# Scores of two attention batches in seven chunks of 128 queries instead of eight of 120

## The chip, the cores and the metric

The kernel runs on one core of a Trainium2 chip. The metric is the time of one execution on the device, in microseconds (us). Before the change the median of three runs was 487.84 us, the lowest 485.43 and the highest 489.74.

## The reference

One attention block with head mixing, then two feed-forward blocks. Everything is fp32, with batch B = 2, H = 12 heads, S = 448 tokens and D = 64 per head.

```
scores = einsum('bhij,hg->bgij', q @ k^T / 8, w_pre)      # mix heads
attn   = softmax(scores, axis=-1)
attn   = einsum('bhij,hg->bgij', attn, w_post)            # mix heads again
x      = (attn @ v) as [B, S, 768]
u      = x + (relu(x^T @ w_tok1) @ w_tok2)^T              # over tokens
x      = u + relu(u @ w_ch1) @ w_ch2                      # over channels
h      = gelu(x @ w_in);  u, v = halves of h
out    = x + (u * (w_sg @ layernorm(v) + b_sg)) @ w_out
```

The change touches only how the raw scores q @ k^T are cut and when their operands are loaded.

## The kernel before, in words

**Scores (`qk`).** The 448 queries of a batch are cut into chunks of 120, 120, 120 and 88, so there are eight chunks for the two batches. For each of them `qk(x, i)` computes chunk x of head pair i: TensorE (PE) multiplies the q columns of the chunk with k of that pair (lines 326 to 329), and one copy on ScalarE (ACT) or VectorE (DVE) takes the result, 128 x 896, out of PSUM into the chunk's S tile (line 333). A call costs the same for the chunk of 88 queries as for one of 120, since the 128 columns of the q tile are filled up with zeros. There are 8 x 6 = 48 calls. S tiles live in three places: one named S3 and two that rotate.

**Steps.** The mixing works on 20 queries at a time: there are 23 steps for each batch, 46 in all, numbered over both batches. For step i:

- `b_dma` gathers the scores from S into two ring tiles P: 10 queries x 12 heads land on 120 partitions. Such a tile is one DMA on the queue of SyncE (SP), and reads 10 rows of S that lie 12 partitions apart. The ring has 8 tiles, four steps' worth. P of step i + 5 is sent in step i, in steps 14 and 16 one step more (`LONG`).
- `b_pre` mixes heads (PE, "pre"), `b_max` finds the negated maximum (DVE, "nm", line 373), `b_exp` exponentiates (ACT, "E", line 381): these three are issued two steps ahead (`LP` = 2).
- `b_norm` forms the weights from the sums (GpSimd, POOL, "wt"), one step ahead.
- `b_post` mixes heads again on PE ("post"), and `b_turn` copies the result into AT, on DVE, in five steps on ACT (line 433).

Two pairs of PSUM banks (`psB`) hold pre; two others (`psM`) are shared in turn by `qk`, post and `av`.

**What lies between the steps.** `av` multiplies AT with v, for two chunks at a time, in steps 12, 14, 16, then 23, 25, 27, then 35, 36, 40 and later. In the middle of `av`, PE waits for a small POOL instruction (`turned_at`, line 474), which in turn waits for the first matmuls of `av`. `QK_AT` gives the step in which each `qk` call stands; in a step the order is pre, `qk`, post, `av` on PE. `CONV` says how many instructions of a conversion of weights are issued in a step: first right after `b_norm`, then after `b_turn` and before `av`, then at the end of the step. Each of four early weight pieces goes through |x| on ACT, a clamp on POOL (line 132), three bit operations on DVE (lines 134, 136, 138), a copy on ACT and a subtraction on POOL. Its raw tile (`eraw`) has one buffer, so the load of the next piece waits on SP until the third DVE operation is done. The list `loads` names the step in which q, k and v are loaded, all on the SP queue in the order of the program.

**After the steps** come the feed-forward blocks, nearly all matmul, and their weights' loads and conversions; they follow the attention part in program order and are not touched by the change.

Of the kernel before, what the change touches and what calls it, by code (L numbers as in the profile page):

```python
# [21 lines left out]
NP_BUFS = 2 * (LD - LP + 1)  # L22
# [3 lines left out]
V_EARLY = {7: 0, 11: 1, 15: 2, 19: 3}  # L26

GATE_ORDER = "u0 u1 v4 u2 v5 u3"


@with_exitstack
def tile_kernel(ctx, tc, q, k, v, w_pre, w_post, w_tok1, w_tok2, w_ch1, w_ch2,
                w_u, w_v, g_ln, w_sg, b_sg, w_out, out):
    nc = tc.nc
    B, D, H, S = 2, 64, 12, 448
    P = 128
    NP = H // 2
# [7 lines left out]
    IB = 10  # L45
    TILES = P // IB
# [235 lines left out]
    def big(nm, dt=F32R):  # L282
        return sp_.tile([P, SWC], dt, tag="S", name=nm, bufs=2)
# [22 lines left out]
    def load_q(b, c, g, eng=nc.sync):
        t = qn[b, c, g] = qp.tile([P, QG, P], F32, tag=f"qn{g}", name=f"qn{b}_{c}_{g}", bufs=2)
        eng.dma_start(out=t, in_=q[b, :, c, g * QG:(g + 1) * QG])

    KG = [(i, 1) for i in range(NP)]  # L310

    def load_k(b, g):
        i, n = KG[g]
        x = qp.tile([P, n, S], F32, tag=f"kn{g}", name=f"kn{b}_{g}")
        nc.sync.dma_start(out=x, in_=k[b, :, i:i + n])
        for j in range(n):
            KX[b, i + j] = x[:, j]

    def qk(x, i, pool=psM, copies=(nc.scalar.copy,)):

        b, c = chunks[x]
        if i == 0:
            SS[b, c] = qp.tile([P, SWC], F32, tag="S3", name=f"S{b}_{c}") if x % 3 == 1 else big(f"S{b}_{c}", F32)
        nm = f"qk{b}_{c}_{i}"
        ps = pair(nm, pool)
        for cols in HALVES:
            for j, rows in enumerate(HALVES):
                nc.tensor.matmul(ps[cols, j, :S], lhsT=qn[b, c, i // QG][rows, i % QG, cols], rhs=KX[b, i][rows],  # L328
                                 start=True, stop=True)
        n = 2 // len(copies)  # L330
        for j, copy in enumerate(copies):
            o = (2 * i + j * n) * S
            copy(SS[b, c][:, o:o + n * S].rearrange("p (j s) -> p j s", j=n), ps[:, j * n:(j + 1) * n, :S])  # L333


    steps = []
# [11 lines left out]
    PAD = 64 - HW  # L348
    NK = S // 64

    ring = [ap_.tile([P, S], F32, name=f"P{n}") for n in range(NP_BUFS)]

    def b_dma(i):

        b, c, p, ne = steps[i]
        for r in range(2):
            t = 2 * p + r
            ni = IB if ne == 2 else HB
            src = SS[b, c][t:t + (ni - 1) * TILES + 1:TILES]
            nc.sync.dma_start(out=ring[(2 * i + r) % NP_BUFS][PAD:PAD + ne * HW], in_=src)  # L360

    def b_pre(i):
        ne = steps[i][3]
# [155 lines left out]
        extra.setdefault(step, []).append((fn, a))  # L519

    chunks = [(b, c) for b in range(B) for c in range(len(CH))]
    NCH = len(chunks)
    starts = set(first.values())


    load_k(0, 0)
    load_q(0, 0, 0, nc.scalar)
    for g in range(1, len(KG)):
        load_k(0, g)
        if g == 2:  # L530
            load_q(0, 0, 1)
    for g in range(NQ):
        load_q(0, 1, g)
    load_const()
    load_v(0, 0)

# [33 lines left out]
    for at, fn, *a in [(1, load_q, 0, 3, 0), (5, load_q, 0, 3, 1), (9, load_k, 1, 0), (10, load_q, 1, 0, 0), (11, load_k, 1, 1),   # L570
                       (12, load_v, 0, 1), (12, load_k, 1, 2), (12, load_k, 1, 3), (12, load_q, 1, 0, 1), (14, load_v, 0, 2),
                       (14, load_k, 1, 4), (14, load_k, 1, 5), (14, w_dma), (14, load_const_late),
                       (16, load_q, 1, 1, 0), (16, load_q, 1, 1, 1), (18, load_q, 1, 2, 0), (20, load_q, 1, 2, 1), (25, load_v, 1, 0), (25, load_q, 1, 3, 0),
                       (27, load_v, 1, 1), (27, load_q, 1, 3, 1), (35, load_v, 1, 2)]:
# [381 lines left out]
def layouts(q, k, v, w_pre, w_post, moe_w_tok1, moe_w_tok2, moe_w_ch1, moe_w_ch2,  # L956
            moe2_w_in, moe2_g_ln, moe2_w_sg, moe2_b_sg, moe2_w_out):

    import numpy as np

    def bits(a):

        return a.view(np.uint64) if a.dtype == np.float64 else a

    def rows(a, p):

        return bits(a).reshape(-1, p, a.shape[1]).transpose(1, 0, 2)

    def blocks(a):

        n = a.shape[0] // 128 * 128
        return rows(np.concatenate([a, a[n:]]), 128)

    def cols(a, p):

        return bits(a).reshape(a.shape[0] // p, p, -1, p).transpose(1, 2, 0, 3)

    def diagonal(w):
        h = w.shape[0]
# [5 lines left out]
    def spread(a):

        n = a.shape[-1]
        full, rest = n // 10, n % 10
        a = a.reshape(*a.shape[:-1], 2, n // 2)
        a = np.concatenate([a, np.zeros((*a.shape[:-1], -(n // 2) % 5), a.dtype)], -1)  # L990
        a = a.reshape(*a.shape[:-1], -1, 5)
        t = np.zeros((*a.shape[:-3], 128), a.dtype)
        rows = t[..., :120].reshape(*a.shape[:-3], 2, 5, 12)
        rows[..., :full] = a[..., :full, :].swapaxes(-1, -2)
        if rest:
            rows[..., 0, :, full:full + 2] = a[..., full, :].swapaxes(-1, -2)
        t[..., :120] = rows.reshape(*a.shape[:-3], 120)
        return t
# [8 lines left out]
    qt = np.stack([spread(qt[..., s:s + 120]) for s in range(0, S, 120)], 2)  # L1007
# [27 lines left out]
    return {n: np.ascontiguousarray(a) for n, a in arrays.items()}  # L1035
# [34 lines left out]
```

## Time and profile before

| | |
|---|---|
| median of three runs | 487.84 us (485.43 to 489.74) |
| the profiled execution's own time | 486.01 us |
| its span, first to last instruction | 484.2 us |
| PE busy | 470.1 us, 97% |
| DVE, ACT, POOL busy | 70%, 48%, 44% |
| granted TensorE clock | 1.0 of full speed throughout |

The times of instructions are microseconds from the span's start. The steps of the attention part run from 14 us to 165 us; what follows lasts to 484 us. "Idle before" in a row of the timeline is how long the engine had nothing to do before that instruction, and after the arrow stands what ended the idle time. Matmul ends are modelled, so a PE that shows as busy may still issue more slowly than it could. "issue" means that no wait shows in the profile. 1.8 us of the 486.01 lie outside the span.

### The profile page before, as it was taken

To read this page: it belongs to the slowest core of one execution; us is meant where nothing else is said; L and a number is where in the kernel's file an instruction comes from. 1 tells how busy PE (TensorE), PEld (TensorE's weight loads), DVE (VectorE), ACT (ScalarE), POOL (GpSimd) and SP (SyncE) were. 2 spreads that over 40 slices of the span, in tenths; PEclk is the share of its full clock that TensorE was granted. 3 is DMA by queue.
4 is the path that set the end of the run, shared out by engine and by line. 5 is a ranking of instruction groups with operands and counts; after the bars stand their busy time and mean duration, and the time that the engine had idled before them with its cause. 6 is when DMAs were issued, how large, how long until landed. Compare 5 with 4: busy or idle time off the path is not lost.

```text
span 484.2 us, 12943 instructions
## 1 busy us (share of the span) xinstructions
PE 470.1 (97%) x5476; PEld 386.8 (80%) x5476; DVE 340.3 (70%) x453; ACT 232.3 (48%) x453; POOL 212.8 (44%) x305
## 2 busy tenths in 40 slices
PE   8979999999999999999999999999999999999997
PEld 4555555566657899999999999999999998888896
DVE  3779556757765568536577767888779855898882
ACT  3767667678764454533344342324333343555320
POOL 2266545756654203831233331655544450358400
PEclk9999999999999999999999999999999999999999
DMA  7656765385635014022243343324333233004222
GB/s 254 238 207 216 274 229 188 112 271 189 231 139 203 5 39 146 12 66 70 104 140 111 134 160 130 132 93 146 132 110 108 85 79 121 21 0 131 81 91 102
DMA packets 26302, 64.17 MB, mean 133 GB/s; under 512 B 2900, under 2 KB 19844, under 8 KB 26244
## 3 DMA queue, kind: packets, MB, share of 16 engines
q1 hardware_dynamic: 26100, 63.14, 38.2%
q8 instruction: 43, 0.70, 0.6%
q10 hardware_dynamic: 144, 0.20, 0.1%
q14 instruction: 15, 0.12, 0.1%
HBM read 41.22 MB, written 2.75 MB: 91 GB/s over the span
## 4 chain that ended last, share of the span: by engine, by line
PE 87%; ACT 3%; issue 3%; DVE 3%; POOL 2%; DMA 2%; POOLq 0%; ACTq 0%; SPq 0%; DVEq 0%
PE qk L328 7%; PE c1ps L673 6%; PE c2ps L673 6%; PE pre L368 6%; PE c2ps L675 6%; PE c1ps L675 6%; PE c2ps L674 6%; PE c1ps L674 6%; PE av L482 6%; PE post L415 5%; PE ups L674 2%; PE ups L673 2%; PE ups L675 2%; PE vps L675 2%; PE vps L673 2%
## 5 line engine op out<-in xcount | busy, mean ns | idle before, releaser
L157 POOL TENSOR_TENSOR wl<-cv,wh 128x768 fp32r<-128x768 f32 x28 | 53.1, 1898 | 124.4 <-ACT wh L154 92.7
L415 PEld LDWEIGHTS post<-wt,E 60*64 60x64 f32 x2520 | 45.3, 134 | 28.1 <-issue 12.3
L381 ACT ACTIVATE E<-pre,nm 128x448 f32<-128x448 f32 x90 | 56.5, 637 | 14.6 <-DVE nm L373 13.0
L415 PE MATMUL post<-wt,E 60*64 60x60 f32 x2520 | 48.5, 219 | 4.9 <-issue 3.5
L136 DVE SCALAR_TENSOR_TENSOR cv<-raw,cv 128x768 uint32<-128x768 uint32 (+2 forms) x44 | 51.5, 1171 | 1.3
L673 PE MATMUL c2ps<-r1h,wh 128*128 128x448 f32 x144 | 52.3, 363 | 0.0
L673 PE MATMUL c1ps<-uh,wh 128*128 128x448 f32 x144 | 52.3, 363 | 0.0
L675 PE MATMUL c2ps<-r1h,wl 128*128 128x448 f32 x144 | 52.2, 362 | 0.0
L675 PE MATMUL c1ps<-uh,wl 128*128 128x448 f32 x144 | 52.2, 362 | 0.0
L674 PE MATMUL c2ps<-r1l,wh 128*128 128x448 f32 x144 | 51.9, 360 | 0.0
L674 PE MATMUL c1ps<-ul,wh 128*128 128x448 f32 x144 | 51.8, 360 | 0.0
L433 DVE COPY AT<-post 128x840 f32<-128x840 f32 x40 | 41.3, 1032 | 14.5 <-PE post L415 14.5
L373 DVE TENSOR_REDUCE nm<-pre 128x2 f32<-128x896 f32 (+1 forms) x46 | 48.9, 1063 | 2.3 <-PE pre L368 2.2
L114 ACT ACTIVATE cv<-raw 128x768 f32<-128x768 f32 (+2 forms) x44 | 36.2, 823 | 28.4 <-POOL wl L157 20.7
L333 ACT COPY S<-qk 128x896 f32<-128x896 f32 x40 | 36.1, 906 | 22.9 <-PE qk L328 22.7
L328 PE MATMUL qk<-kn,qn 64*64 64x448 f32 x384 | 45.7, 555 | 1.5 <-DMA qn<-in_q_dram 1.5
L368 PE MATMUL pre<-P,wp 64*64 64x448 f32 (+1 forms) x360 | 46.1, 539 | 0.3 <-ACT E L381 0.3
L138 DVE SCALAR_TENSOR_TENSOR cv<-raw,cv 128x768 uint32<-128x768 uint32 (+2 forms) x44 | 41.9, 952 | 1.1
L154 ACT CAST wh<-cv 128x768 fp32r<-128x768 f32 x28 | 23.4, 836 | 34.8 <-DVE cv L138 33.8
L696 DVE SCALAR_TENSOR_TENSOR r1l<-c1ps,r1h 128x448 fp32r<-128x448 f32 x24 | 15.0, 623 | 30.6 <-ACT r1h L694 30.6
L134 DVE TENSOR_SCALAR cv<-cv 128x768 uint32<-128x768 uint32 (+2 forms) x44 | 30.4, 692 | 6.8 <-POOL turned_at L474 3.0
L390 POOL TENSOR_TENSOR rr<-rc,mone 128x2 f32<-128x2 f32 (+1 forms) x46 | 33.4, 726 | 3.8
(151 smaller groups left out, 997.1 us busy)
## 6 DMA issues: line engine op xcount, KB each, us to landing
P<-S SPq DMA_DIRECT2D x88, 210.0 KB
raw<-in_w_ch_dram SPq DMA_DIRECT2D x24, 768.0 KB
vn<-in_v_dram SPq DMA_DIRECT2D x6, 512.0 KB
raw<-in_w_v_dram SPq DMA_DIRECT2D x6, 512.0 KB
raw<-in_w_u_dram SPq DMA_DIRECT2D x4, 768.0 KB
raw<-in_w_out_dram SPq DMA_DIRECT2D x6, 512.0 KB
qn<-in_q_dram SPq DMA_DIRECT2D x15, 192.0 KB
kn<-in_k_dram SPq DMA_DIRECT2D x12, 224.0 KB
```

The lines of the kernel that those rows point to most:

```text
L136: nc.vector.scalar_tensor_tensor(fi, lo, 29, fi, op0=ALU.logical_shift_right, op1=ALU.bitwise_or)
L138: nc.vector.scalar_tensor_tensor(fi, hi, 0xC0000000, fi, op0=ALU.bitwise_and, op1=ALU.bitwise_or)
L157: nc.gpsimd.tensor_tensor(dst[1], f, f32(dst[0]), op=ALU.subtract)
L328: nc.tensor.matmul(ps[cols, j, :S], lhsT=qn[b, c, i // QG][rows, i % QG, cols], rhs=KX[b, i][rows], start=True, stop=True)
L368: nc.tensor.matmul(ps[cols, e, :S], lhsT=wp[rs], rhs=ring[(2 * i + r) % NP_BUFS][rs], start=True, stop=True)
L373: nc.vector.tensor_reduce(out=st[i]["nm"][:, :ne], in_=st[i]["pre"][:, :ne, :S], axis=AX.X, op=ALU.max, negate=True)
L381: nc.scalar.activation(t, st[i]["pre"][:, e, :S], AF.Exp, bias=st[i]["nm"][:, e:e + 1], scale=1.0, accum_out=sm[:, e:e + 1])
L415: nc.tensor.matmul(ps[HALVES[x], r, o:o + HW], lhsT=st[i]["e"][e][rs, t * 64:(t + 1) * 64], rhs=st[i]["w"][e][rs, :HW], start=True, stop=True)
L433: copy(dst, src)
L673: nc.tensor.matmul(ps, lhsT=lh, rhs=rh, start=(start and i == 0), stop=False)
L674: nc.tensor.matmul(ps, lhsT=lh, rhs=rl, start=False, stop=False)
L675: nc.tensor.matmul(ps, lhsT=ll, rhs=rh, start=False, stop=(stop and i == n - 1))
```

## The change

The queries of both batches are laid in one row of 896 and cut into seven chunks of 128. Chunk 3 holds the last 64 queries of batch 0 and the first 64 of batch 1, so its `qk` calls take k of both batches. There are 7 x 6 = 42 calls. The steps stay as they were. A P tile whose 10 queries lie in two chunks is gathered by two DMAs; `score_rows` lists the places. This happens for the tiles whose queries are split 8 + 2, 6 + 4, 4 + 6 (batch 0) and 4 + 6, 2 + 8 (batch 1): 97 gathers in place of 92. In batch 0 the last five whole tiles read rows 5 partitions apart, in batch 1 the first six read rows 6 apart; the pieces of a split tile, and the two short tiles at the end of each batch, read neighbouring rows. The two short tiles are 48 rows of P in place of 60.

While chunk 3 is computed, k of both batches must be held. The first three pairs of k of batch 1 are loaded into tiles that the weight conversion uses later (`eraw` and `ecv`, "lent"), the other three over pairs of batch 0 that are done; the first three are loaded a second time in steps 16 and 17. k is then loaded in steps 7, 9, 10, 11, 12, 12, 16, 16, 17 instead of 9, 11, 12, 12, 14, 14, one load of q chunk (two DMAs) falls away, and the conversions move from steps 15 to 42 into steps 22 to 41. The host's reordering of q follows `score_rows`.

The core of the diff:

```
     def load_k(b, i, home):
+        if home < 0:
+            if not lent:
+                lent[0] = ap_.tile([P, 2 * EC], U32, tag="eraw", name="lent0").bitcast(F32)
+                lent[1] = ap_.tile([P, EC], F32, tag="ecv", name="lent1")
+            x = (lent[0][:, :S], lent[0][:, EC:EC + S], lent[1][:, :S])[home]
+        else:
+            x = qp.tile([P, S], F32, tag=f"kn{home}", name=f"kn{b}_{i}")
+        nc.sync.dma_start(out=x, in_=k[b, :, i])
+        KX[b, i] = x
...
-        for cols in HALVES:
+        for h, cols in enumerate(HALVES):
...
-                nc.tensor.matmul(ps[cols, j, :S], lhsT=qn[b, c, i // QG][rows, i % QG, cols], rhs=KX[b, i][rows],
+                nc.tensor.matmul(ps[cols, j, :S], lhsT=qn[x, i // QG][rows, i % QG, cols],
+                                 rhs=KX[(2 * x + h) // NCH, i][rows], start=True, stop=True)
...
         for r in range(2):
-            t = 2 * p + r
-            ni = IB if ne == 2 else HB
-            src = SS[b, c][t:t + (ni - 1) * TILES + 1:TILES]
-            nc.sync.dma_start(out=ring[(2 * i + r) % NP_BUFS][PAD:PAD + ne * HW], in_=src)
+            to = PAD
+            for x, a, by, n in places(b, c, 2 * p + r):
+                src = SS[x][a:a + (n - 1) * by + 1:by]
+                nc.sync.dma_start(out=ring[(2 * i + r) % NP_BUFS][to:to + n * H], in_=src)
+                to += n * H
...
-    QK_AT = [[-2, -2, -1, -1, 0, 1], [3, 5, 7, 9, 11, 12], [13, 14, 14, 15, 16, 17], [18, 18, 19, 20, 21, 22], [23, 24, 25, 26, 27, 28], [29, 30, 31, 32, 33, 34]]
+    QK_AT = [[-2, -2, -1, -1, 0, 1], [9, 11, 12, 13, 14, 14], [15, 16, 17, 18, 19, 20], [21, 22, 23, 24, 25, 26], [28, 29, 30, 31, 32, 33]]
...
-    CONV = {15: (0, 0, 2), 16: (0, 3, 0), 18: (1, 0, 0), 19: (0, 1, 0), 21: (0, 1, 0), 22: (1, 1, 0), 23: (0, 2, 0), 25: (0, 0, 1), 26: (1, 0, 0), 27: (2, 3, 0), 29: (0, 1, 0), 30: (1, 0, 0), 36: (1, 1, 0), 38: (1, 0, 1), 39: (0, 1, 0), 40: (1, 0, 0), 42: (0, 0, 1)}
-    RAW_AT = (16, 23, 27)
+    CONV = {22: (0, 0, 1), 23: (1, 3, 1), 24: (1, 0, 0), 25: (1, 0, 1), 27: (0, 3, 1), 28: (1, 0, 0), 35: (1, 0, 1), 36: (0, 3, 1), 37: (1, 0, 0), 39: (0, 0, 1), 40: (1, 3, 1), 41: (1, 0, 0)}
+    RAW_AT = (17, 23, 27, 36)
```

`qk` calls therefore disappear from steps 3, 5, 7, 27 and 34, and step 18 keeps one of its two; every other step from 9 to 33 keeps the number that it had.

## Rows read from the trace of the kernel before

**Rows 1.** The page: busy time of each engine, and the chain's shares.
```profile
PE 470.1 (97%) x5476; PEld 386.8 (80%) x5476; DVE 340.3 (70%) x453; ACT 232.3 (48%) x453; POOL 212.8 (44%) x305
PE 87%; ACT 3%; issue 3%; DVE 3%; POOL 2%; DMA 2%; POOLq 0%; ACTq 0%; SPq 0%; DVEq 0%
```

**Rows 2.** The page's groups: busy us, mean ns of one | idle before, releaser.
```profile
L373 DVE TENSOR_REDUCE nm<-pre 128x2 f32<-128x896 f32 (+1 forms) x46 | 48.9, 1063 | 2.3 <-PE pre L368 2.2
L433 DVE COPY AT<-post 128x840 f32<-128x840 f32 x40 | 41.3, 1032 | 14.5 <-PE post L415 14.5
...
L333 ACT COPY S<-qk 128x896 f32<-128x896 f32 x40 | 36.1, 906 | 22.9 <-PE qk L328 22.7
L328 PE MATMUL qk<-kn,qn 64*64 64x448 f32 x384 | 45.7, 555 | 1.5 <-DMA qn<-in_q_dram 1.5
```

**Rows 3.** Windows: stretch, length, PE, PEld, DVE, ACT, POOL busy, clock, DMA, GB/s.
```profile
25.35:45.53 20.18, 17.18 (x548) 11.04 (x544) 16.30 (x17) 14.14 (x39) 12.30 (x33) 1.00 0.57 205
67.84:74.81 6.97, 5.77 (x116) 3.58 (x116) 4.47 (x7) 3.03 (x8) 5.69 (x10) 1.00 0.50 154
74.81:78.43 3.62, 3.26 (x84) 1.62 (x77) 2.62 (x3) 3.20 (x7) 0.96 (x3) 1.00 0.32 122
104.26:106.58 2.32, 2.32 (x76) 1.39 (x72) 1.87 (x3) 2.07 (x5) 1.01 (x1) 1.00 0.66 234
106.58:112.51 5.93, 5.72 (x116) 3.46 (x113) 2.91 (x7) 3.97 (x10) 5.23 (x10) 1.00 0.59 175
124.39:129.29 4.90, 4.12 (x140) 2.93 (x139) 3.27 (x4) 3.49 (x8) 3.07 (x8) 1.00 0.49 185
165.00:484.00 319.00, 315.12 (x1702) 289.57 (x1697) 230.59 (x320) 123.56 (x198) 124.06 (x89) 1.00 0.29 97
```

**Rows 4.** Timeline, 23 to 33 us: start, length, instruction, count [idle before].
```profile
23.48 0.49 SPq L308 DMA_DIRECT2D qn<-in_q_dram  x1
...
28.16 0.98 PE L328 MATMUL qk<-kn,qn 64*64 64x448 f32 x8 [0.80 <-DMA qn<-in_q_dram]
...
32.87 0.63 PE L415 MATMUL post<-wt,E 60*64 60x60 f32 x28 [1.79 <-issue]
```

**Rows 5.** Timeline around the `av` of step 16.
```profile
67.80 0.69 ACT L114 ACTIVATE cv<-raw 128x512 f32<-128x512 f32 x1
...
68.57 1.93 POOL L132 TENSOR_SCALAR cv<-cv 128x512 f32<-128x512 f32 x1 [4.82 <-ACT cv L114]
...
69.33 0.44 PE L464 MATMUL av<-AT,vn 64*64 64x120 f32 x8 [0.50 <-ACT S L333]
...
73.05 0.44 PE L464 MATMUL av<-AT,vn 64*64 64x120 f32 x8 [0.70 <-POOL turned_at L474]
```

**Rows 6.** Timeline of PE, steps 26 and 27.
```profile
105.83 0.94 PE L328 MATMUL qk<-kn,qn 64*64 64x448 f32 x8
106.58 1.00 PE L415 MATMUL post<-wt,E 60*64 60x60 f32 x56
107.79 0.44 PE L464 MATMUL av<-AT,vn 64*64 64x120 f32 x8 [0.21 <-ACT S L333]
```

**Rows 7.** Timeline, steps 33 to 35.
```profile
125.57 0.85 PE L415 MATMUL post<-wt,E 60*64 60x60 f32 x43 [0.78 <-issue]
...
128.84 1.04 DVE L433 COPY AT<-post 128x840 f32<-128x840 f32 x1 [0.29 <-PE post L415]
...
130.10 0.32 PE L464 MATMUL av<-AT,vn 64*64 64x120 f32 x3
```

**Rows 8.** Timeline of the SP queue's gathers and loads, and two `qk` calls.
```profile
19.98 3.45 SPq L360 DMA_DIRECT2D P<-S  x4
...
36.70 1.63 SPq L360 DMA_DIRECT2D P<-S  x2
...
42.69 1.02 PE L328 MATMUL qk<-kn,qn 64*64 64x448 f32 x8
...
45.66 0.47 SPq L308 DMA_DIRECT2D qn<-in_q_dram  x1
...
49.69 0.96 PE L328 MATMUL qk<-kn,qn 64*64 64x448 f32 x8
```

More of the change, by code (lines that the diff above doesn't have):

```diff
@@ L28, with score_rows @@
 GATE_ORDER = "u0 u1 v4 u2 v5 u3"
+def score_rows():
+    S, IB, P = 448, 10, 128
+    got = []
+    for b in range(2):
+        sizes = [IB] * (S // IB) + [S % IB // 2] * 2
+        at, rows = b * S, [[] for _ in sizes]
+        t = done = 0
+        while t < len(sizes):
+            room = P - at % P
+            left = sizes[t] - done
+            full = 0
+            while not done and sizes[t] == IB and t + full < S // IB and (full + 1) * IB <= min(room, (b + 1) * S - at):
+                full += 1
+            if full:
+                for n in range(full):
+                    rows[t + n].append((at + n, full, IB))
+                at += full * IB
+                t += full
+                continue
+            n = min(left, room)
+            rows[t].append((at, 1, n))
+            at += n
+            done += n
+            if done == sizes[t]:
+                t, done = t + 1, 0
+        got.append(rows)
+    return got
 @with_exitstack
@@ L299, in tile_kernel @@
     QG = 3
+    NCH = B * S // P
     NQ = NP // QG
@@ L304, in load_v, with load_q, load_k @@
         nc.sync.dma_start(out=t, in_=v[b, :, g])
[L306 to L317, printed above, removed]
+    def load_q(x, g, eng=nc.sync):
+        t = qn[x, g] = qp.tile([P, QG, P], F32, tag=f"qn{g}", name=f"qn{x}_{g}", bufs=2)
+        eng.dma_start(out=t, in_=q[x, :, g * QG:(g + 1) * QG])
+    lent = {}
+    def load_k(b, i, home):
+        if home < 0:
[7 more added lines that the diff above has]
+        KX[b, i] = x
     def qk(x, i, pool=psM, copies=(nc.scalar.copy,)):
-        b, c = chunks[x]
         if i == 0:
-            SS[b, c] = qp.tile([P, SWC], F32, tag="S3", name=f"S{b}_{c}") if x % 3 == 1 else big(f"S{b}_{c}", F32)
-        nm = f"qk{b}_{c}_{i}"
-        ps = pair(nm, pool)
-        for cols in HALVES:
+            SS[x] = qp.tile([P, SWC], F32, tag="S3", name=f"S{x}") if x % 3 == 0 else big(f"S{x}", F32)
+        ps = pair(f"qk{x}_{i}", pool)
+        for h, cols in enumerate(HALVES):
             for j, rows in enumerate(HALVES):
-                nc.tensor.matmul(ps[cols, j, :S], lhsT=qn[b, c, i // QG][rows, i % QG, cols], rhs=KX[b, i][rows],
-                                 start=True, stop=True)
+                nc.tensor.matmul(ps[cols, j, :S], lhsT=qn[x, i // QG][rows, i % QG, cols],
+                                 rhs=KX[(2 * x + h) // NCH, i][rows], start=True, stop=True)
         n = 2 // len(copies)
@@ L332, in qk @@
             o = (2 * i + j * n) * S
-            copy(SS[b, c][:, o:o + n * S].rearrange("p (j s) -> p j s", j=n), ps[:, j * n:(j + 1) * n, :S])
+            copy(SS[x][:, o:o + n * S].rearrange("p (j s) -> p j s", j=n), ps[:, j * n:(j + 1) * n, :S])
     steps = []
@@ L349, in tile_kernel, with places @@
     NK = S // 64
+    def places(b, c, t):
+        return [(n // P, n % P, by, m) for n, by, m in score_rows()[b][TILES * c + t]]
     ring = [ap_.tile([P, S], F32, name=f"P{n}") for n in range(NP_BUFS)]
@@ L521, in tile_kernel @@
     chunks = [(b, c) for b in range(B) for c in range(len(CH))]
-    NCH = len(chunks)
     starts = set(first.values())
[L526 to L531, printed above, removed]
+    load_k(0, 0, 0)
+    load_q(0, 0, nc.scalar)
+    for i in range(1, NP):
+        load_k(0, i, i)
+        if i == 2:
+            load_q(0, 1)
     for g in range(NQ):
-        load_q(0, 1, g)
+        load_q(1, g)
     load_const()
@@ L567, in tile_kernel @@
     for g in range(NQ):
-        load_q(0, 2, g)
+        load_q(2, g)
     loads = {}
[L570 to L574, printed above, removed]
+    for at, fn, *a in [(1, load_q, 3, 0), (5, load_q, 3, 1), (7, load_k, 1, 0, -3), (9, load_k, 1, 1, -2), (10, load_q, 4, 0), (10, load_k, 1, 2, -1),
+                       (11, load_k, 1, 3, 0), (12, load_k, 1, 4, 1), (12, load_v, 0, 1), (12, load_k, 1, 5, 2), (12, load_q, 4, 1), (14, load_v, 0, 2),
+                       (14, load_const_late), (16, load_k, 1, 0, 3), (16, load_k, 1, 1, 4), (16, load_q, 5, 0), (17, load_k, 1, 2, 5),
+                       (18, load_q, 5, 1), (25, load_v, 1, 0), (23, load_q, 6, 0),
+                       (27, load_v, 1, 1), (25, load_q, 6, 1), (35, load_v, 1, 2)]:
         loads.setdefault(at, []).append((fn, a))
@@ L590, in tile_kernel @@
     todo = []
-    for x in range(0, NCH - 2, 2):
+    for x in range(0, len(chunks) - 2, 2):
         f0, f1 = first[chunks[x + 2]], first[chunks[x + 3]]
         for m in range((NP // 2)):
-            todo.append((f0 + (MID_AT[m] if x + 4 == NCH else m * (f1 - f0) // (NP // 2)), chunks[x:x + 2], (2 * m, 2 * m + 1)))
+            todo.append((f0 + (MID_AT[m] if x + 4 == len(chunks) else m * (f1 - f0) // (NP // 2)), chunks[x:x + 2], (2 * m, 2 * m + 1)))
     for m, hps in enumerate(LAST):
@@ L983, in diagonal @@
         return t
[L985 to L998, printed above, removed]
     def tokens(w):
@@ L1006, in layouts @@
     qt = q.reshape(B, H // 2, 2, S, D).transpose(0, 2, 4, 1, 3).reshape(B, 2 * D, H // 2, S)
-    qt = np.stack([spread(qt[..., s:s + 120]) for s in range(0, S, 120)], 2)
+    order = np.zeros(B * S, int)
+    for b, tiles in enumerate(score_rows()):
+        for t, segments in enumerate(tiles):
+            c, j = t // 12, t % 12
+            n = min(120, S - 120 * c)
+            rows_at = np.concatenate([np.arange(a, a + by * m, by) for a, by, m in segments])
+            i = np.arange(len(rows_at))
+            if t < S // 10:
+                order[rows_at] = b * S + 120 * c + i // 5 * (n // 2) + 5 * j + i % 5
+            else:
+                r = t - S // 10
+                order[rows_at] = b * S + 120 * c + r * (n // 2) + n // 10 * 5 + i
+    qt = qt.transpose(1, 2, 0, 3).reshape(2 * D, H // 2, B * S)[..., order].reshape(2 * D, H // 2, -1, 128).transpose(2, 0, 1, 3)
     whole = S // 128 * 128
```

## The prediction

> **What bounds the kernel now.** I read the page's busy lines first, then the groups by operation, then windows laid over single stretches, then the timeline inside them. PE is busy 97% of the span and carries 87% of the chain [rows 1], and after 165 us PE is busy for 315.12 of 319.00 us [rows 3]. The change takes nothing out of that part, so it only starts earlier by whatever the attention part gives up; the whole gain or loss must be found between 14 and 165 us. There a busy PE is not enough to go by. A plain step with one `qk` call takes 2.32 us (the window from 104.26 [rows 3]), and PE is recorded busy through all of it. But DVE needs 1.063 us for its maximum and 1.032 us for the copy into AT [rows 2], 2.10 us for every step, call or no call. So a call taken out of a plain step can give at most about 0.22 us before DVE sets the pace, though its PE slot is 0.75 us long (105.83 to 106.58 [rows 6]). The first stretch shows the same: eight steps in 20.18 us [rows 3], less the idle 0.80 and 1.79 us [rows 4], are 2.20 us a step, although about half of them have a call. Six calls at 45.7 us / 48 = 0.95 us of PE each [rows 2], 5.7 us, is therefore not the forecast; each call is worth what its own step can give.
>
> **The six calls that go.**
>
> Step 3: PE stands 0.80 us for the q chunk whose load went out at 23.48 [rows 4]. In the new order that chunk is first used in step 9, so the wait goes. Soon after, PE is idle 1.79 us with no wait that the profile names [rows 4]; if that idle time hangs on the clock on the wall and not on the work before it, it swallows the gain. Bounds 0 and 0.8; I take 0.7, since a wait that is named is gone for certain and the other is not known to move. Next late there is DVE.
>
> Steps 3, 5, 7: from 2.20 to at best 2.10 us over the eight steps, 0.8 at most, 0 at least; I take 0.3.
>
> Step 18: two calls in one step make 3.62 us (the window from 74.81 [rows 3]), a step with one 2.32. Gain 1.3; a second call in a step is pure PE and ACT time (its copy takes 0.906 us [rows 2]), and DVE is busy only 2.62 of the 3.62.
>
> Step 27: here `av` follows. The call's slot is 0.75 us, and `av` then waits 0.21 us more, because it takes over the call's PSUM pair and must wait for its copy [rows 6]. Without the call it follows post directly: 0.96 us. DVE is busy 2.91 of 5.93 us in the `av` stretch (the window from 106.58 [rows 3]) and doesn't step in. I take 1.0; lower bound 0.2, if DVE's pace carries through.
>
> Step 34: before the last steps without calls, two steps last 4.90 us (the window from 124.39 [rows 3]), of which 0.78 is idle without a named cause [rows 7]. `av` starts at 130.10, 0.2 us after the copy into AT that ends at 129.88 [rows 7], so DVE is again close behind. Bounds 0.2 and 0.75 + 0.78 = 1.5; I take 0.6, nearer the end that DVE's row gives.
>
> **The conversions.** In step 16 the clamp on POOL (1.93 us) stands ahead of the fence of `av`, which keeps PE 0.70 us, and |x| on ACT delays the copy that `av` needs, so it starts after 0.50 us instead of 0.21 [rows 5, 6]. The stretch is 6.97 against 5.93 us [rows 3]. No conversion stands there in the new order: 1.0 gained. The new places are the slots of the old step 27: clamp right after `b_norm`, DVE operations ahead of `av`, and that stretch shows 5.93 us with all of it inside; DVE's idle 3 us there are the cover. If the clamps of steps 23 and 40 came late, each would cost 0.70. The |x| at the end of step 22 stands as it stood in step 15: 0.3 lost. The subtractions on POOL only change their steps: 0.
>
> **The loads of k.** Chunk 3 is first multiplied in step 9, and k for it goes out in steps 7, 9 and 10. In the old trace the load of step 7 would follow the gathers that end at 38.3, and one extra gather, so it goes out at about 39.3; PE wants it at 42.69 [rows 8]. That of step 10 follows a q load that ends at 46.13, for a call at 49.69 [rows 8]. The one load that PE waited for took 28.0 - 23.5 = 4.5 us, behind gathers sent without pause [rows 4]. By that both come about 1.1 us late; if the queues are emptier, neither does. Bounds 0 and 2.2, plus what a faster start takes off the margin; I take 0.5, because the gathers around these loads have pauses between them [rows 8]. In step 12 the load into the third pair's place waits on SP for the call of the same step; behind it stand a q load and the gathers for step 18, six steps ahead. `av` of that step covers it.
>
> **The gathers.** Four of them in a row take 3.45 us on SP, 0.86 each [rows 8]; five more are 4.3 us of SP. They are sent five steps, over 10 us, ahead of use: 0 on the path, with rival A as the other end. Half a chunk's q load and three k loads more or less cancel.
>
> **Sum.** 0.7 + 0.3 + 1.3 + 1.0 + 0.6 + 1.0 - 0.3 - 0.5 = 4.1 us. Against the profiled execution, 486.01 us, that is 481.9. That run lies 1.8 under the median of the three; against the median, 487.84, the forecast is **483.7 us**.
>
> **Rivals.**
>
> *A, the split gathers are slow and k comes late: slower than before.* A gather now reads 10 rows 12 partitions apart; a piece of a split tile reads 2 to 8 neighbours. 0.86 us is the most that the spread one can need, since four follow each other at that pace [rows 8]. [...] Net of 4.6 gained, 1 to 3 us are lost: 489.8 in the middle. It decides as soon as the two pieces take over 5 us together. For it: nothing else in the trace has so few source rows. Against it: the stop is bounded by one load, and gathers themselves have steps to spare. [...] Chance 0.17.
>
> *B, DVE and the chain through it bound every plain step.* Then steps 3, 5, 7, 34 give nothing and step 27 only 0.2; 1.3 + 0.2 + 1.0 - 0.3 - 0.5 = 1.7: 486.1. For it: the 2.20 us of the first stretch. Against it: the named 0.80 us. Chance 0.20.
>
> *C, the idle time without a cause goes too.* 1.79 and 0.78 us [rows 4, 7] fall in stretches that lose calls; 4.1 + 2.6 = 6.7: 481.1. Against it: fewer PE instructions don't say where such idle time falls next. Chance 0.17.
>
> That all six calls and their copies go is plain from the loop, so no rival doubts it. The forecast keeps 0.46.
>
> **Range and chances.** 1% is 4.9 us, about what a measurement of this kernel can tell, since its own three runs lie 4.3 us apart. C and the forecast's upper terms pass it: faster 0.29. Slower by 1% takes 9 us of new waits, rival A at its worst: 0.07. Within 1%: 0.64. The range reaches from just under C, 480.4, to the middle of B and A, 488.6; the forecast's own is 481.5 to 486.
>
> **What would show it.** In the new trace: 42 calls; `av` of step 16 without the wait for `turned_at`; no stretch of 3.62 us in step 18; plain steps without a call at 2.1 to 2.2 us; the calls of steps 9, 11 and 12 with an idle time ended by a load of k of under 1 us in all; the feed-forward part of unchanged length. Waits of several us for kn or P in steps 6 to 13 would prove A. A first stretch of steps 2 to 10 that still lasts 20 us, with the 0.80 gone, would say B.

## The result, and the profile after

The changed kernel takes 494.09 us (median of 5 runs, 493.63 to 494.76), against 487.84 before; on one chip the ratio is 1.0136, with a 95% interval of 1.0100 to 1.0173. It is **slower by 6.6 us** where a gain of 4.1 was forecast, and lies outside the predicted range of 480.4 to 488.6. Below, 1% of a ratio is 4.87 us (the kernel before took 486.9 beside the first experiments, 486.4 to 487.2 beside the others).

The page of the changed kernel: busy time, the chain, granted clock, and the groups that answer to [rows 1, 2].

```profile
PE 472.9 (96%) x5428; PEld 389.2 (79%) x5428; DVE 341.3 (69%) x453; ACT 228.1 (46%) x447; POOL 212.9 (43%) x305
PE 84%; DMA 4%; ACT 4%; DVE 3%; issue 2%; POOL 2%; SPq 0%; POOLq 0%; ACTq 0%
L412 DVE TENSOR_REDUCE nm<-pre 128x2 f32<-128x896 f32 (+1 forms) x46 | 49.0, 1065 | 5.9 <-PE pre L407 3.6
L472 DVE COPY AT<-post 128x840 f32<-128x840 f32 x40 | 41.3, 1031 | 16.6 <-PE post L454 16.5
```

48 PE instructions are gone (six calls of eight each), yet PE is busy 2.8 us longer: the granted clock was 0.50 from 45.5 to 52.3 us, where PE is busy for 5.5 us. DMA has doubled its share of the chain, from 2 to 4%.

Windows of the changed kernel over the same work as [rows 3] (columns as there). A step is counted from the first matmul of its post to that of the next; the first window goes from post of step 2 to post of step 10, the last is the feed-forward part:

```profile
25.81:50.96 25.15, 19.65 (x524) 12.72 (x524) 16.35 (x17) 12.30 (x37) 12.71 (x34) 0.89 0.60 195
73.80:82.53 8.73, 5.71 (x117) 3.62 (x117) 2.68 (x4) 2.58 (x7) 3.19 (x9) 1.00 0.57 157
82.53:84.85 2.32, 2.32 (x77) 1.37 (x73) 1.85 (x3) 2.08 (x5) 0.00 (x0) 1.00 0.76 228
113.80:115.37 1.57, 1.57 (x68) 1.16 (x64) 1.15 (x2) 1.32 (x2) 0.00 (x0) 1.00 0.51 190
115.37:120.85 5.48, 5.48 (x116) 3.51 (x112) 4.07 (x8) 3.93 (x12) 4.11 (x10) 1.00 0.71 178
133.60:137.62 4.02, 3.72 (x133) 2.34 (x129) 3.48 (x4) 2.60 (x6) 2.62 (x7) 1.00 0.21 76
172.00:491.00 319.00, 316.22 (x1733) 290.46 (x1732) 232.56 (x323) 124.72 (x202) 123.66 (x89) 1.00 0.30 97
```

Line by line against [rows 3]: the first eight steps 25.15 for 20.18 us; step 16 8.73 for 6.97; the old double call 2.32 for 3.62; the next two together 7.05 for 8.25; the two steps of the last call 4.02 for 4.90; the last part unchanged (from the last post to the end of the span 320.2 us for 320.5). So the stretches of the calls of steps 18, 27 and 34 give what was forecast, and the largest losses stand in the first stretch, 5.0 us, and in step 16, 1.8. Smaller ones lie beside them: steps 18 to 22 take 12.9 us for 11.6, step 23 6.6 for 6.0, step 25 7.1 for 5.9, and steps 28 to 32 12.8 for 11.9.

The changed kernel, around the first call of chunk 3 (step 9), SP's queue and PE:

```profile
38.02 2.38 SPq L398 DMA_DIRECT2D P<-S  x3
40.45 2.34 SPq L352 DMA_DIRECT2D lent<-in_k_dram  x1
46.79 1.01 PE L362 MATMUL qk<-lent,qn 64*64 64x448 f32 x2 [3.64 <-DMA lent<-in_k_dram]
```

and its windows there:

```profile
42.00:46.70 4.70, 1.15 (x12) 0.14 (x2) 1.77 (x2) 0.91 (x4) 2.23 (x7) 0.87 0.52 155
46.70:51.00 4.30, 4.21 (x69) 3.20 (x73) 0.88 (x1) 2.15 (x5) 0.17 (x1) 0.50 0.66 223
```

The two pieces of step 12's split tile stand right ahead of the first lent load of k. Such a load occupied SP for 0.39 to 0.51 us in the kernel before, in one case for 1.88; this one holds it for 2.34, and k comes 3.64 us late. Then a second price is added: PE, idle in most of the first window, works on at a granted clock of 0.50. From post of step 8 to that of step 12 the kernel takes 15.8 us instead of 9.4. Step 16 has the second wait, for the third piece of v:

```profile
71.52 1.49 SPq L335 DMA_DIRECT2D vn<-in_v_dram  x1
77.82 0.43 PE L503 MATMUL av<-AT,vn 64*64 64x120 f32 x8 [3.02 <-DMA vn<-in_v_dram]
```

### The profile page after: what moved, and what is told of

Read it like the earlier page. It is cut to its first block, busy times and chain, and to the rows that moved or that the text cites. A ratio compares the mean times of both kernels' runs of the same rounds, so it can differ in the third digit from the quotient of the medians.

```text
span 492.2 us, 12842 instructions
## 1 busy us (share of the span) xinstructions
PE 472.9 (96%) x5428; PEld 389.2 (79%) x5428; DVE 341.3 (69%) x453; ACT 228.1 (46%) x447; POOL 212.9 (43%) x305
## 4 chain that ended last, share of the span: by engine, by line
PE 84%; DMA 4%; ACT 4%; DVE 3%; issue 2%; POOL 2%; SPq 0%; POOLq 0%; ACTq 0%
PE qk L362 6%; PE c1ps L711 6%; PE c2ps L711 6%; PE c2ps L713 6%; PE c1ps L713 6%; PE c2ps L712 6%; PE c1ps L712 6%; PE av L521 6%; PE pre L407 5%; PE post L454 5%; PE ups L712 2%; PE ups L711 2%; PE ups L713 2%; PE vps L713 2%; PE vps L712 2%
## 5 line engine op out<-in xcount | busy, mean ns | idle before, releaser
L454 PEld LDWEIGHTS post<-wt,E 60*64 60x64 f32 x2520 | 48.8, 138 | 24.9 <-POOL wt L433 10.4
L454 PE MATMUL post<-wt,E 60*64 60x60 f32 x2520 | 51.1, 223 | 2.9 <-POOL wt L433 1.6
L711 PE MATMUL c1ps<-uh,wh 128*128 128x448 f32 x144 | 52.3, 363 | 0.0
L711 PE MATMUL c2ps<-r1h,wh 128*128 128x448 f32 x144 | 52.3, 363 | 0.0
L407 PE MATMUL pre<-P,wp 64*64 64x448 f32 (+1 forms) x360 | 50.5, 551 | 1.5 <-DMA P<-S 0.8
L367 ACT COPY S<-qk 128x896 f32<-128x896 f32 x34 | 30.7, 907 | 27.0 <-PE qk L362 26.7
L362 PE MATMUL qk<-kn,qn 64*64 64x448 f32 x300 | 38.4, 563 | 0.9 <-DMA qn<-in_q_dram 0.9
L427 POOL TENSOR_SCALAR rc<-sm 128x2 f32<-128x2 f32 (+1 forms) x46 | 10.9, 237 | 64.1 <-ACT E L420 63.5
```

Of the source, the lines that this page charges most:

```text
L362: nc.tensor.matmul(ps[cols, j, :S], lhsT=qn[x, i // QG][rows, i % QG, cols], rhs=KX[(2 * x + h) // NCH, i][rows], start=True, stop=True)
L407: nc.tensor.matmul(ps[cols, e, :S], lhsT=wp[rs], rhs=ring[(2 * i + r) % NP_BUFS][rs], start=True, stop=True)
L454: nc.tensor.matmul(ps[HALVES[x], r, o:o + HW], lhsT=st[i]["e"][e][rs, t * 64:(t + 1) * 64], rhs=st[i]["w"][e][rs, :HW], start=True, stop=True)
L711: nc.tensor.matmul(ps, lhsT=lh, rhs=rh, start=(start and i == 0), stop=False)
```

## The experiments

Theory N: the rows of the split gathers lie side by side and are therefore slow (rival A of the prediction). Theory Q: it is only the order on SP's queue, an early enough load mends it. M, in the expectations, is wider than Q: only the number of transfers or the margin between load and use is at fault, and the rows do not matter. From the sixth experiment on the question is what took the gain that was forecast in the other terms.

**1. k early.**

```
-(7, load_k, 1, 0, -3), (9, load_k, 1, 1, -2), (10, load_q, 4, 0), (10, load_k, 1, 2, -1)
+(5, load_k, 1, 0, -3), (6, load_k, 1, 1, -2), (8, load_k, 1, 2, -1), (10, load_q, 4, 0)
```

> The changed kernel with one thing moved: the three loads of k into lent places go out in steps 5, 6 and 8 in place of 7, 9 and 10, so the first two stand ahead of the 6 + 4 split gather on the SP queue. Theory N (gathers of neighbouring rows are slow and hold up what is queued behind them): the wait for k in step 9 (3.64 us idle, and the granted clock of 0.5 from 45.5 to 52.3 us after it) goes, steps 8 to 11 take 9.5 to 10.5 us in place of 15.8, the whole 488 us; P of steps 7 to 9 is late by up to 1 us more. Rival M (only the margin between load and use was too small, rows do not matter): the same gain here, so this run gives the price of the wait and does not tell the two apart. If the wait cost only its own idle time: 490.5 us.

Measured 494.69 us, ratio 1.0143 (1.0089 to 1.0196): no gain. The wait for k in step 9 is gone; two others came instead. PE with idle over 1 us before it:

```profile
47.30 0.59 PE L407 MATMUL pre<-P,wp 60*64 60x448 f32 x1 [1.35 <-DMA P<-S]
63.56 0.59 PE L362 MATMUL qk<-kn,qn 64*64 64x448 f32 x2 [1.06 <-DMA kn<-in_k_dram]
```

The wait for v in step 16 stays, with 3.23 us, and this time the granted clock fell to 0.50 after it. Here the delay moved along the queue: in place of 3.64 us for k in step 9, PE waits 1.35 us for a P tile and 1.06 for a later k.

**2. v early.** `(14, load_v, 0, 2)` becomes `(13, load_v, 0, 2)`.

> The changed kernel with the load of v's third group in step 13 in place of 14, ahead of the gathers that wait for the last score call of the middle chunk. Theory Q (on the SP queue the load stood behind a gather that waits for a score copy of step 14): the 3.02 us of idle before av in step 16 goes, 491 us. Rival: the load is late because the DMA engines are held up by slow gathers; then moving it 5 us forward on the queue gains under 1 us: 493.5 us.

Measured 496.27 us, 1.0186 (1.0143 to 1.0230). Step 16 falls from 8.73 to 5.91 us, but these remain or come:

```profile
47.28 1.01 PE L362 MATMUL qk<-lent,qn 64*64 64x448 f32 x2 [4.52 <-DMA lent<-in_k_dram]
90.43 1.80 PE L407 MATMUL pre<-P,wp 64*64 64x448 f32 x6 [2.34 <-DMA P<-S]
```

After both the granted clock fell to 0.50. Q's mends work where they are made and not on the total.

**3. All rows apart.** Every gather reads as many rows 12 apart, so this kernel mixes scores of the wrong queries where the tiles were split or their rows 5 or 6 apart; gathers, bytes and order stay.

```
 for x, a, by, n in places(b, c, 2 * p + r):
+    if by != TILES:
+        a, by = (2 * p + r) % TILES, TILES
```

> The changed kernel, in which every gather that read neighbouring rows or rows 5 or 6 apart reads as many rows 12 apart in the same chunk: same number of DMAs, same bytes, same order; the rows are the wrong ones, so the scores of these queries are not the reference's. Theory N: the wait for P before step 8 (0.83 us), most of the wait for k in step 9 (3.64 us idle to under 1.5), the half clock after it and the slow stretch of steps 18 to 22 go; 486 to 488 us. Rival M (too many DMAs or too little margin): 493 to 495 us, as the changed kernel.

Measured 486.51 us, 0.9985 (0.9952 to 1.0018), the clock at 1.0. The same number of gathers and bytes, other rows, and 7.4 us less than the changed kernel (1.0136 - 0.9985 = 1.51%). Theory N stands, M falls. Of the waits for k one of 0.56 us is left:

```profile
43.32 0.59 PE L362 MATMUL qk<-lent,qn 64*64 64x448 f32 x2 [0.56 <-DMA lent<-in_k_dram]
```

The stretch in which the tile of step 6 (8 + 2) is gathered, first in the changed kernel, then here:

```profile
24.00:27.00 3.00, 3.00 (x128) 2.23 (x128) 2.71 (x3) 2.38 (x7) 1.80 (x6) 1.00 0.49 77
```

```profile
25.00:28.00 3.00, 3.00 (x132) 2.08 (x128) 2.71 (x4) 2.57 (x7) 1.69 (x5) 1.00 0.60 206
```

The DMA engines are occupied in both, but move 77 GB/s in the one and 206 in the other (last two columns). In the packet records, 1,792-byte packets take 74 ns in the median; between 22 and 28 us the slowest tenth takes over 253 ns in the changed kernel, 74 with the rows apart.

**4. Neighbouring rows in the kernel before.** The chunk of batch 1's queries 240 to 359 is laid out so that each of its tiles reads 10 neighbouring rows; q is reordered to match.

```
+if (b, c) == (1, 2):
+    src = SS[b, c][IB * t:IB * t + IB]
```

> The kernel before, with one edit: in the third chunk of batch 1 (steps 35 to 40, gathers sent in steps 30 to 35) each tile's 10 queries lie on 10 neighbouring rows in place of 10 rows 12 apart; the values stay right. Theory N: a gather that took at most 0.86 us takes 2.5 to 3.4 us, the 12 of them 30 to 40 us in place of 10, PE waits for P in steps 35 to 40 by 10 to 25 us in all; 500 us or more. Rival M: rows do not matter, 487 to 489 us, no wait for P.

A single run: 492.61 us, against a median of 486.92 (single runs from 484.1 to 491.89). By that run twelve tiles of 92 cost 5.7 us. These twelve on SP's queue, and PE's named wait for one:

```profile
116.90 22.84 SPq L362 DMA_DIRECT2D P<-S  x12
148.74 1.31 PE L370 MATMUL pre<-P,wp 64*64 64x448 f32 x6 [2.23 <-DMA P<-S]
```

and windows of it:

```profile
122.00:126.00 4.00, 3.08 (x55) 1.80 (x58) 2.08 (x2) 0.73 (x4) 2.26 (x7) 0.75 0.52 117
134.00:140.00 6.00, 6.00 (x138) 4.12 (x133) 3.14 (x4) 2.69 (x7) 4.37 (x9) 1.00 0.54 112
```

1.90 us for a gather, not 0.86 [rows 8], and not the 2.5 to 3.4 of the expectation, which no run shows; and again half the rate at a busy share of over one half (before, 118 to 126 us: 229 and 255 GB/s). The expectation had the sign right and was too high: the twelve take 12.5 us more of SP's queue than at 0.86 each (22.84 - 10.3), and the time rose by 5.7; the queue's five steps of lead may have taken the rest. In its trace step 31 alone lost 2.8 us, where an idle of PE without a named cause (1.94 us) and a slower clock (0.75 in the mean from 122 to 126 us) fall together.

**5. Only the pieces and short tiles apart.** The condition of the third experiment becomes `by == 1`.

> The changed kernel, but only the pieces of split tiles and the short tiles (14 gathers) read their rows 12 apart; the tiles with rows 5 and 6 apart stay as they are (the scores of the tiles moved are wrong). Theory 1, only neighbouring rows are slow because they pass through one place: as with all rows apart, 486 to 488, PE's wait of 3.64 us for k in step 9 shrinks to under 1, the granted clock stays at 1.0. Theory 2, every spacing under 12 is slow (22 tiles with rows 5 or 6 apart): half or more of the loss stays, 490 to 494.

Measured 489.18 us (single runs from 486.42 to 494.88), 1.0052 (1.0023 to 1.0081). Between the theories: 1.0136 - 1.0052 = 0.84%, 4.1 us, come from the neighbouring rows (2.3 either way), and 1.0052 - 0.9985 = 0.67%, 3.3 us, from rows 5 and 6 apart (2.1 either way). There are 11 such tiles, not the 22 of the expectation. What PE still waits for:

```profile
51.35 0.59 PE L362 MATMUL qk<-lent,qn 64*64 64x448 f32 x2 [1.00 <-DMA lent<-in_k_dram]
72.14 0.44 PE L505 MATMUL av<-AT,vn 64*64 64x120 f32 x8 [1.64 <-DMA vn<-in_v_dram]
```

**6. The conversions alone**, in the kernel before: `CONV` and `RAW_AT` of the change, and without `(14, w_dma)`.

> The kernel before with the conversions in the places of the changed one (step 22 to 41, raw loads in steps 17, 23, 27, 36) and nothing else. The prediction's terms: +1.0 in step 16, -0.3 in step 22, so 0.7 faster: about 486.2 against 486.9. Rival, from the run with rows apart, where step 16 gained 1.06 but steps 23 and 36 to 45 lost 0.66 and 1.16: 0.5 to 1.0 slower, 487.5 to 488.

Measured 485.20 us, 0.9978 (0.9957 to 0.9999): 1.1 us faster, near the prediction's term of 0.7, but hardly clear of nothing. Step 16 and step 23 there:

```profile
70.00 0.44 PE L464 MATMUL av<-AT,vn 64*64 64x120 f32 x8 [0.21 <-ACT S L333]
70.36 2.65 PE L482 MATMUL av<-AT,vn 128*64 128x240 f32 x24
72.95 0.44 PE L464 MATMUL av<-AT,vn 64*64 64x120 f32 x8
```

```profile
91.18:97.68 6.50, 6.21 (x120) 3.81 (x124) 4.26 (x8) 3.73 (x10) 5.90 (x9) 1.00 0.14 31
```

The fence costs nothing in step 16 any more, which lasts 5.91 for 6.97 us; step 23 pays back half, 6.50 for 5.96. Steps 40 and 41 pay the rest, first in the kernel before, then here, where `av` of step 40 waits 0.36 us for `turned_at` behind the clamp:

```profile
145.19:154.01 8.82, 8.82 (x228) 6.84 (x232) 5.22 (x8) 4.42 (x13) 4.64 (x14) 1.00 0.73 276
```

```profile
144.72:154.21 9.49, 9.12 (x228) 6.94 (x232) 6.07 (x10) 4.96 (x14) 7.50 (x15) 1.00 0.66 244
```

By these steps the conversions gain nothing (1.06 - 0.54 - 0.67 = -0.15 us). Where the median's 1.1 us come from the trace doesn't show: its execution took 487.0 us, the longest of the twelve.

**7. The six calls put back**, in the kernel with all rows apart.

```
+for at, *call in [(3, 3, 0, psM, (nc.scalar.copy,), 0), (5, 3, 1, ...), (7, 3, 2, ...),
+                  (18, 4, 3), (27, 6, 0), (34, 6, 5)]:
+    scores.setdefault(at, []).append(call)
```

> The kernel with all rows apart, and the six score calls put back in steps 3, 5, 7, 18, 27 and 34 (their results are overwritten or repeated, so they add work and change no score). If the calls are worth what the prediction said (0.3 + 1.3 + 1.0 + 0.6, without the wait for q): 3.2 us slower than with rows apart, 489.5 to 490. If something else paces these steps and takes back what a call leaves: within 1 us of 486.5.

Measured 490.43 us, 1.0088 (1.0054 to 1.0122). Against the third experiment that is 1.03%, 5.0 us, with 2.3 either way, more than the 3.2 expected but within its error. Not all of it is the calls: the wait for q is back in step 2 (0.73 us), and step 25, which got no call, takes 9.73 us for the 7.01 with rows apart, with 2.31 us of unnamed idle (last section). With the calls, and with no slow rows, this kernel is still 4.3 us behind the one before, in its trace 3.8 of them in step 25.

**8. Rows apart, conversions in the old places**, k loaded a second time in steps 13 and 14.

> The kernel with all rows apart, and the conversions in the places of the kernel before (steps 15 to 42; for that the three k of the lent tiles are loaded a second time in steps 13 and 14 instead of 16 and 17). If the moved conversions hide about 1 to 2 us of the gain: 484.5 to 485.5. If the prediction's +0.7 for them holds: 487.2. If idle time of PE without a named cause takes whatever is gained: 486 to 487.

Measured 494.10 us, 1.0172 (1.0141 to 1.0203); none had this. The first raw weight piece, sent at 67.7 us, lands at 75.3, ACT waits for it ahead of |x| until then, and `av` of step 16 waits 4.28 us for a copy behind it. As a test of the conversions it fails: it moved loads as well.

**9 to 12. The instruction stream.** In the kernel before all of PE's unnamed idle times over 0.4 us end 1.4 to 1.5 us after a packet of queue q8, an instruction queue by the page. By its 43 packets for PE's 10,952 matmuls and weight loads, 255 to a packet, it is taken for the one that brings PE's instructions. These four put 128 (or 64) more PE instructions ahead: 37 (or 21) idle multiplications of 8 columns in place of 5 of 128, in the kernel before (9), with rows apart (10, and 12 with 64), and with the conversions alone (11).

> The kernel before, with the 5 idle multiplications of 128 columns at the start replaced by 37 of 8 columns: 128 more PE instructions ahead of everything, no other change. Theory F, PE's unnamed idle times hang on where its instruction stream is fetched (each followed a fetch of 256 instructions by 1.4 to 1.5 us): the idle of 1.8 us in step 4 goes or moves to another step, and the median moves by 0.5 to 2 us either way from 486.4. Rival, the idle belongs to the steps themselves: same steps, same lengths, median within 0.5 us.

> The kernel with all rows apart, and the same 128 more PE instructions at the start. Theory F: its unnamed idle (6.5 us in all, 2.16 of it in step 10) falls on other steps, and with an average hand (about 3.5, as in the kernel before) the median is 483 to 485 instead of 486.2. Rival: 486 to 487, the same idle in the same steps.

> The kernel before with the conversions in the new places only, and the same 128 more PE instructions at the start. Theory F: idle in other steps (there 0.85 and 0.69 us in steps 4 and 6, 1.43 in step 42), median 484 to 487 against 485.2 without the shift. Rival: 485.2 within 0.5.

> The kernel with all rows apart, and 64 more PE instructions at the start instead of 128. Theory F: again another set of steps, and a median that differs from that with 128 by 0.5 to 2 us. Rival: both alike, 486 to 487.

Measured 500.50, 500.25, 500.42 and 494.55 us. The medians can't be read as meant: the small multiplications were far from free, and the first post comes at 34.0, 34.2, 34.9 and 27.6 us instead of 21.4. But the idle did move. The 1.79 us of [rows 4] is not in the shifted kernel before, which has this in step 30 instead:

```profile
132.94 0.46 PE L415 MATMUL post<-wt,E 60*64 60x60 f32 x16 [1.96 <-issue]
```

So these times don't belong to a step. Nor does the place in the stream settle them alone: experiments 13 and 14 below run the same PE instructions as the kernel before, and neither has an idle of over 0.3 us in step 4. That the shifted kernels with and without the change end alike (500.25 and 500.50, each ratio with 0.45% either way) leaves open how much of a gain they take.

**13. Five more gathers** in the kernel before: the same tiles in two pieces, all rows 12 apart.

```
+for n in {(6, 0): (8, 2), (12, 1): (6, 4), (19, 0): (4, 6), (26, 0): (4, 6), (32, 1): (2, 8)}.get((i, r), (ni,)):
```

> The kernel before, with the same five tiles split in two gathers of 8 + 2, 6 + 4 or 4 + 6 rows, all 12 apart: 97 gathers in place of 92, nothing else. The prediction's term (0 on the path): within 1 us of 486.4. If the number of gathers is what takes the gain that is missing: 488.5 to 490.

Measured 486.31 us, 0.9980 (0.9963 to 0.9997): the number of gathers costs nothing. This trace has 0.9 us of unnamed idle where that of the kernel before has 3.5, none of it in steps 2 to 8 or 33 and 34, so it shows what these stretches take with their calls and without such idle (the third row is steps 2 to 8 of the third experiment, without the calls):

```profile
27.84:40.89 13.05, 12.69 (x412) 7.16 (x409) 12.19 (x13) 10.50 (x30) 9.27 (x25) 1.00 0.64 225
124.28:128.30 4.02, 4.02 (x141) 2.54 (x137) 3.45 (x4) 3.67 (x10) 2.85 (x8) 1.00 0.62 221
```

```profile
26.99:39.61 12.62, 10.88 (x389) 6.25 (x385) 11.89 (x13) 7.80 (x25) 9.22 (x25) 1.00 0.69 228
```

**14. Three more loads of k** in the kernel before.

```
+(7, load_lent, 1, 0), (9, load_lent, 1, 1), (10, load_lent, 1, 2)
```

> The kernel before, with three more loads of k in steps 7, 9 and 10, into the places that the changed kernel lends (nothing reads them). If the loads in that stretch take the gain that is missing: 488.5 to 490, with waits of PE between steps 7 and 13. If not: within 1 us of 486.4.

Measured 491.28 us, 1.0078 (1.0049 to 1.0107): **3.8 us slower**. Its named waits are not where the loads are, but steps later:

```profile
69.21 0.98 PE L337 MATMUL qk<-kn,qn 64*64 64x448 f32 x8 [1.93 <-DMA kn<-in_k_dram]
73.22 0.44 PE L473 MATMUL av<-AT,vn 64*64 64x120 f32 x8 [2.21 <-ACT S L342]
```

The second is again |x| on ACT (71.71) that waits for its raw piece. The same 15 us in the kernel before, and then here:

```profile
40.00:55.00 15.00, 14.80 (x417) 9.35 (x413) 11.31 (x12) 10.72 (x28) 10.46 (x28) 1.00 0.76 253
```

```profile
40.00:55.00 15.00, 13.37 (x325) 8.47 (x321) 8.89 (x10) 9.20 (x24) 8.54 (x24) 1.00 0.88 243
55.00:74.00 19.00, 14.18 (x344) 8.43 (x338) 8.03 (x10) 10.86 (x23) 5.17 (x12) 1.00 0.79 240
```

DMA already moved 253 GB/s before; with more to do its busy share rises to 0.88 and the rate doesn't. Three loads of 224 KB are 0.69 MB, 2.8 us at 243 GB/s, by which what stands behind them would come later. That the engines were full is argued from the rate alone: in other stretches the kernel before moves more, 276 GB/s in the window shown in experiment 6. And this is not the price of the changed kernel's loads: it has six loads of k in steps 7 to 14, as many as the kernel before, and its three more come in steps 16 and 17. Here nine stand in steps 7 to 14.

**15. Rows apart, k and v early** (the edits of 1 and 2 in 3).

> The kernel with all rows apart, with the lent loads of k in steps 5, 6 and 8 and the third load of v in step 13. If late loads take the missing gain: PE waits for no k or v, and 483 to 484.5. If idle time without a named cause takes it wherever the loads stand: 486 to 487.5.

Measured 486.33 us, 0.9977 (0.9951 to 1.0003). No wait for k or v is left, and it is no clear gain on the third experiment. PE's longest idle is unnamed, in the middle of post of step 19:

```profile
80.33 0.87 PE L456 MATMUL post<-wt,E 60*64 60x60 f32 x45 [1.67 <-issue]
```

**16. Pieces and short tiles from ACT's queue**, in the changed kernel: `(nc.scalar if by == 1 else nc.sync).dma_start(...)`.

> The changed kernel, right in all values, with the 14 gathers of neighbouring rows sent from ACT's queue in place of SP's. If a slow piece costs by holding up what stands behind it on SP: k and v come in time, 487 to 489.5 as with the pieces apart. If it costs wherever it is sent from, since its rows pass through one place and the others wait there too: 492 to 495.

Measured 503.84 us, 1.0343 (1.0311 to 1.0376), beyond what either said. PE waits six times about 1 to 3 us for pieces or short tiles, of which two, and the sending of the first piece:

```profile
34.28 2.51 PE L407 MATMUL pre<-P,wp 64*64 64x448 f32 x5 [2.38 <-DMA P<-S]
132.57 0.82 PE L407 MATMUL pre<-P,wp 64*64 64x448 f32 x2 [2.94 <-DMA P<-S]
27.96 1.29 ACTq L398 DMA_DIRECT2D P<-S  x1
```

Off SP the pieces come still later. That doesn't tell a slow piece from one that is sent late: ACT sends the first at 27.96 us, 3.4 us after the first post, where SP in the changed kernel sent it at 22.18, 0.4 us after it. Why the other queue is so much worse stays open.

## Why the prediction was wrong, point by point

**The gathers: "0 on the path, with rival A as the other end".** This step failed, and it is the largest: 7.4 us, with 2.4 either way, between the changed kernel and the one with rows apart. Rival A had it, at a chance of 0.17: the split gathers are slow and k comes late; the wait of several us for k that was to prove it is there, in step 9. With 4.6 gained, its loss of 1 to 3 us makes a price of 5.6 to 7.6. That is near the 7.4, but by luck: no run shows the time of a piece from which this price, A's 489.8 and with it the upper end of the range were worked out. The runs show 1.90 us for a gather of ten neighbours where one with rows 12 apart takes 0.86, and 3.64 us for the wait in step 9; three things that the price left out come on top of the wait. A mended wait came back at other transfers (1.35 us for P and 1.06 for k in experiment 1, 2.34 for P in experiment 2). PE's idle time was followed by a stretch at half clock: the granted clock was 0.50 from 45.5 to 52.3 us, PE worked in 5.5 us of these, and at half speed that is up to 2.7 us more (not after every wait: through step 16, with 3.02 us of it, the clock stayed 1.00). And rows 5 and 6 apart, which the prediction never mentioned, carry 3.3 of the 7.4.

Why the rows are slow was not shown. The slowest tenth of the 1,792-byte packets took over 253 ns in the changed kernel (22 to 28 us) and over 267 in the fourth experiment (113 to 140 us), where in the kernel before it begins at 74 in both stretches; the packets show that they are slow, not where. In the fifth experiment a quarter of the packets from 60 to 82 us, where the tiles with rows 5 apart are gathered, took over 108 ns, against 74 before, which agrees with the 3.3 us for rows 5 and 6 apart.

**The loads of k: 0.5, "bounds 0 and 2.2".** Outside its bounds in the changed kernel, where the wait took 3.64 us, but through the gathers ahead of the load: with rows apart 0.56 us are left, which is the term. Sending k and v earlier there leaves no wait and gains 0.4 us, with 2.0 either way (experiments 3 and 15). What the prediction had wrong beside it is that "half a chunk's q load and three k loads more or less cancel": a whole chunk of q falls away, two loads of 192 KB, for three of 224. Three more loads in steps 7 to 14 would have cost 3.8 us (2.4 to 5.2, experiment 14); the change has its three in steps 16 and 17, and PE waits for none of them.

**The six calls: 3.9 in all** (0.7 + 0.3 + 1.3 + 1.0 + 0.6). The size was right: 5.0, with 2.3 either way, by experiment 7, and 3.7 by the steps of the traces. The wait for q went, 0.8. Steps 2 to 8 last 12.62 us with rows apart, 2.10 each, which is DVE's pace (maximum and copy, 1.07 + 1.03 us), and 13.05 in experiment 13, with the calls and without a wait for DMA or unnamed idle: 0.4, forecast 0.3. Step 18 gave 1.30 (forecast 1.3), step 27 with the step before it 1.20 (1.0). Step 34 gave 0.88 (0.6), but that was luck: its two steps last 4.02 us without the call in the changed kernel, and 4.02 with it in experiment 13. What went is the idle of 0.78 us, and the call was free; rival B's "nothing" came true there alone.

**The conversions: +0.7.** The median says 1.1 (0.05 to 2.1), the steps nothing. The fence of step 16 gave 1.06 by the trace (forecast 1.0). In step 23 the copy that `av` needs waited 0.55 us behind |x|, where 0.3 was set. And the clamp of step 40 did come late: 0.67 in steps 40 and 41, which the prediction named (0.70) and counted at nothing.

**The sum.** Forecast was a gain of 4.1 us, measured a loss of 6.6: 10.7 apart. The rows are 7.4 of these. By the steps above, the calls (3.7), the conversions (-0.15) and the wait for k (-0.6) leave a gain of 3.0, so 1.1 more are mis-sized terms. The kernel with rows apart shows a gain of 0.7, with 1.6 either way; the 2.3 between that and 3.0 stay open. A candidate is PE's unnamed idle, 3.5 us in the profile of before, 6.5 in that of the third experiment and 0.9 in that of the thirteenth, one execution of each; it was not separated. It may also be what keeps the medians of single edits from adding up: -5.0 (calls), -1.1 (conversions) and -1.0 (gathers in two pieces, 0.1 to 1.8) would make -7.1. Rival C took the unnamed idle to go with the calls; it moved.

## What to carry to other kernels

Price a DMA that gathers rows of SBUF by the partitions it reads, not by its bytes alone: here a gather of ten rows took 0.86 us with the rows 12 apart and 1.90 with neighbouring rows (experiment 4), and 11 tiles with rows 5 or 6 apart cost 3.3 us (experiments 3 and 5). Keep the rows of one transfer apart, or price them from packets. Before loads are added to a stretch, read its GB/s: in experiment 14 the rate did not rise with more to do (253 GB/s before, 243 after), and the waits appeared steps later under other names. Price a wait of PE of several us with the slow clock that can come with it: with the 3.64 us in step 9 it fell to 0.50 for 6.8 us, with the 3.02 in step 16 it stayed 1.00. And read a term of under 2 us from the steps it touches, since idle time without a cause moves between kernels by as much (1.79 us in step 4 of the kernel before, 1.96 in step 30 of experiment 9).

## What was not expected of the hardware

Beside the slow transfers the issuing was slow too: SP needed 2.34 us, behind two slow gathers, for a load of k that took it 0.45 with the rows apart. The engines' busy share doesn't show slow transfers, since 77 and 206 GB/s stand at 0.49 and 0.60. After an idle of PE without a named cause the clock fell as well; the seventh experiment, PE and then a window:

```profile
103.18 0.50 PE L456 MATMUL post<-wt,E 60*64 60x60 f32 x17 [2.31 <-issue]
```

```profile
103.20:107.50 4.30, 4.30 (x47) 2.84 (x49) 1.03 (x1) 0.25 (x2) 3.20 (x5) 0.64 0.81 261
```

After 2.31 us of idle the mean granted clock is 0.64 for the next 4.3 us, and that step takes 9.73 us where it took 5.93 before and 7.01 with rows apart.
